# Linear attention and spectral mixing: attention batches written one ahead, transposes over head pairs, weights fetched later

## The chip, the cores and the metric

The kernel runs on one core of one Trainium2 chip. The metric is device time in microseconds (us) of one execution; lower is better. Where rows come from the hardware profiler, they are of one profiled execution of the kernel before.

## What is computed

The inputs q, k, v have shape 8 x 8 x 576 x 64 (batch, head, sequence, head size), the spectral weights `w_r` and `w_i` 64 x 512 x 512, the channel weights `w_ch` 512 x 512, all float32. The output is 8 x 576 x 512 float32.

```python
def phi(x):
    return np.where(x > 0, x, np.exp(x) - 1.0) + 1.0
q_p, k_p = (phi(q), phi(k))
kv = np.einsum('bhsd,bhse->bhde', k_p, v)
z = np.sum(k_p, axis=2)
num = np.einsum('bhsd,bhde->bhse', q_p, kv)
den = np.einsum('bhsd,bhd->bhs', q_p, z)[..., None] + 1e-06
x = num / den                      # heads side by side: 8 x 576 x 512
X = np.fft.rfft(x, axis=1)         # the first 64 modes are kept
Yr = einsum('bmd,mde->bme', Xr, w_r) - einsum('bmd,mde->bme', Xi, w_i)
Yi = einsum('bmd,mde->bme', Xr, w_i) + einsum('bmd,mde->bme', Xi, w_r)
y = np.fft.irfft(Y, n=S, axis=1)
u = x + y
out = u + np.maximum(u @ w_ch, 0.0)
```

## The kernel before

The program has three parts that follow one another.

**The attention part** (lines 128 to 294) loops over the 8 batches. For each it loads q, k and v (`q16`, `k16`, `v16`: 512 rows of the sequence, cast to half precision by the DMA, issued by POOL) and the last 64 rows (`q_t`, `k_t` in float32, issued by SP; `v16t`). VectorE and ScalarE form phi: a minimum with zero on DVE (L177), an exponential on ACT (L178), and one fused instruction on DVE, (x + 1) max e (L179); L182 to L184 do the same for the 64 tail rows. Then four head pairs follow. For each pair TensorE sums k'v into `kv_ps` (L206, 5 matmuls for each head), DVE copies it (`kv_sb`, L213), TensorE transposes q' into `qT_ps` (L219 and L222, 5 transposes for each head, each writing 64 partitions), ACT copies that (`q_pT`, L225 and L226), TensorE forms numerator and denominator (`num_ps`, L236 and L242), and DVE divides into `x_main` and `x_tail` (L251 to L259). At the batch's end ACT casts x to half precision (`x16m`, `x16t`), TensorE applies a Fourier matrix in five matmuls (`fft`, L273 and L276), ACT copies the result (`xr_sb`), and eight small transposes (`xtps`, L284) bring it into `xt_c`, from which DVE and ACT copy out twice each (L290 to L294).

**The spectral part** (L301 to L355) multiplies, for each of 64 modes, the batch rows of `xt_c` by `w_r` (L317) and `w_i` (L326): 128 weight tiles of 512 x 512, 0.5 MB each in half precision, all issued by POOL (L118, L120) into a pool with `bufs=7`. Every one of these matmuls reads all batches of `xt_c`, so the first stands behind the last batch's attention. `NPREF = 4` modes (8 tiles) are asked for within the batch loop, at batches 0, 2, 4 and 6.

**The last part** (L358 to L396) applies the inverse Fourier matrix (`inv_sb`), adds x, transposes (`utps`, L373), multiplies by `w_ch` (L380) and stores.

The code is written batch by batch, but a scheduler sets the order on each engine when the program is built, by priority and by which buffers are free; each engine then takes its instructions strictly in that order and waits where one isn't ready. POOL's queue counts too: a DMA that waits for a buffer holds up all that stand behind it. Most tiles of the batch loop have two buffers, `q_t`, `k_t`, `v16t` and `scr_t` one. `num_ps`, `fft` and `xtps` share four PSUM buffers.

Of the kernel before, what the change touches and what calls it, by code (L numbers as in the profile page):

```python
# [11 lines left out]
F32 = mybir.dt.float32  # L12
F16 = mybir.dt.float16
BF16 = mybir.dt.bfloat16
# [14 lines left out]
def _fft_consts(S: int, NM: int):  # L29
# [21 lines left out]
    inv = np.concatenate([inv, inv], axis=0)  # L51
# [4 lines left out]
def kernel(  # L56
# [15 lines left out]
    NB = 4  # L72
# [27 lines left out]
    nc.sync.dma_start(out=inv_sb, in_=inv_dr.ap())  # L100
# [15 lines left out]
    def _w_load(kk: int):  # L116
        wr = wpool.tile([128, NDC, D], BF16, tag="w", bufs=7, name=f"wr{kk}")
        nc.gpsimd.dma_start(out=wr, in_=moe_w_r[kk].rearrange("(dc p) e -> p dc e", p=128))  # L118
        wi = wpool.tile([128, NDC, D], BF16, tag="w", bufs=7, name=f"wi{kk}")
# [3 lines left out]
    with (  # L123
# [4 lines left out]
        for b in range(B):  # L128
            if b % 2 == 0 and b // 2 < NPREF:
                w_pref[b // 2] = _w_load(b // 2)  # L130
            q16 = qkv.tile([128, 2, H, 2, Dh], F16, tag="q16", bufs=2, name=f"q16_{b}")
            k16 = qkv.tile([128, 2, H, 2, Dh], F16, tag="k16", bufs=2, name=f"k16_{b}")
            v16 = qkv.tile([128, 2, H, 2, 72], F16, tag="v16", bufs=2, name=f"v16_{b}")
            q_t = qkv.tile([ST, H, Dh], F32, tag="q_t", bufs=1, name=f"q_t{b}")
            k_t = qkv.tile([ST, H, Dh], F32, tag="k_t", bufs=1, name=f"k_t{b}")
            v16t = qkv.tile([ST, H, 72], F16, tag="v16t", bufs=1, name=f"v16t{b}")

            for c in range(2):
                nc.gpsimd.dma_start(
                    out=q16[:, c],  # L140
                    in_=q[b, :, c * 256 : (c + 1) * 256, :].rearrange(
                        "h (s2 par) d -> s2 h (par d)", par=2
                    ),
                )
# [284 lines left out]
```

## Time and profile before

| | |
|---|---|
| six runs, median (lowest to highest) | 594.03 us (593.13 to 595.7) |
| the profiled execution, its own time | 595.7 us |
| its span in the trace | 593.7 us |
| first spectral matmul | 172.98 us |
| last weight tile's matmuls | 491.03 us |
| PE / DVE / ACT busy over the span | 71% / 35% / 22% |

The median is 0.3 us above the span and 1.7 us below the profiled execution's own time. The three parts are read apart, since each has its own limit: the attention part up to 173 us, the weights' stretch up to 491 us, and the last part. Differences between spans stand for differences between times.

### The profile page before, as it was taken

The numbers are of one execution on the slowest core, as the hardware profiler recorded it, in microseconds if no ns is written. First come the engines' busy times: TensorE is split into PE (matmuls) and PEld (weight loads), VectorE is DVE, ScalarE is ACT, GpSimd is POOL, SyncE is SP. The second block draws the span as 40 slices with busy tenths as digits, with TensorE's granted clock in tenths as the row PEclk, the third lists the DMA queues.
The fourth block names the chain that finished last, engine by engine and source line by source line (L and its number), as shares of the span: only waits on it lengthen the run. The fifth ranks groups of instructions, "written<-read, shape, count | busy, mean of one in ns | idle before, by whom it ended". The sixth has DMA issues, their size and how long they took to land.

```text
span 593.7 us, 5577 instructions
## 1 busy us (share of the span) xinstructions
PE 420.0 (71%) x1976; PEld 168.9 (28%) x1976; DVE 209.8 (35%) x529; ACT 131.7 (22%) x218; POOL 158.4 (27%) x205
## 2 busy tenths in 40 slices
PE   0378799999855665656666666767676664999885
PEld 0255465655521111111111111111111111323442
DVE  1485977777511101110110100311011103576653
ACT  1346666665420000000000000000000001502673
POOL 6656444330014222222322222222222200000000
PEclk9999999999997667676766555575655665867998
DMA  9999998983009999999999999999999990004444
GB/s 158 168 186 185 181 169 73 123 78 31 1 8 194 206 206 206 206 206 207 206 206 206 209 210 210 207 206 206 206 207 206 206 183 10 13 13 161 167 173 141
DMA packets 155243, 94.21 MB, mean 159 GB/s; under 512 B 83280, under 2 KB 150480, under 8 KB 155216
## 3 DMA queue, kind: packets, MB, share of 16 engines
q0 software_dynamic: 138896, 80.75, 95.9%
q1 hardware_dynamic: 16320, 13.12, 8.0%
q8 instruction: 15, 0.25, 0.2%
q14 instruction: 12, 0.10, 0.0%
HBM read 164.10 MB, written 9.44 MB: 292 GB/s over the span
## 4 chain that ended last, share of the span: by engine, by line
DMA 55%; PE 27%; issue 10%; DVE 4%; ACT 2%; POOL 1%; SPq 0%; DVEq 0%; POOLq 0%; ACTq 0%
DMA wi<-in_moe_w_i_dram 25%; DMA wr<-in_moe_w_r_dram 22%; PE e L380 6%; DMA q<-in_q_dram 5%; PE y L361 5%; PE P L326 3%; PE qT L219 3%; PE P L317 2%; DMA k<-in_k_dram 2%; PE kvp L206 2%; PE fft L273 1%; PE utp L373 1%; PE num L236 1%; ACT ut L377 1%; PE qT L222 1%
## 5 line engine op out<-in xcount | busy, mean ns | idle before, releaser
L317 PE MATMUL P<-wr,xt_c 128*16 128x512 bf16 x256 | 112.7, 594 | 56.6 <-DMA wr<-in_moe_w_r_dram 55.6
L336 DVE CAST ystage<-P 16x512 bf16<-16x512 f32 x64 | 43.9, 687 | 279.3 <-PE P L326 232.6
L326 PE MATMUL P<-wi,xt_c 128*16 128x512 bf16 x256 | 103.2, 550 | 52.6 <-DMA wi<-in_moe_w_i_dram 52.6
L370 ACT CAST u<-x_main 128x512 f16<-128x512 f32 x32 | 19.1, 624 | 329.7 <-DVE x_main L368 329.6
L120 POOL DMA_DIRECT2D wi<-in_moe_w_i_dram x64 | 47.5, 743 | 138.2 <-PE P L317 138.2
L118 POOL DMA_DIRECT2D wr<-in_moe_w_r_dram x64 | 48.0, 750 | 104.0 <-PE P L326 94.4
L317 PEld LDWEIGHTS <-xt_c 128*16 128x16 bf16 x256 | 30.1, 123 | 138.3 <-issue 115.3
L326 PEld LDWEIGHTS <-xt_c 128*16 128x16 bf16 x256 | 32.2, 126 | 125.2 <-issue 121.0
L219 PE MATMUL qT<-id,qp 128*64 128x128 f16 x256 | 40.1, 312 | 26.9 <-DVE qp L179 23.9
L380 PE MATMUL e<-wch,ut 128*128 128x512 f16 (+1 forms) x160 | 42.5, 406 | 5.7 <-ACT ut L377 4.1
L361 PE MATMUL y<-yg,inv_sb 64*128 64x512 bf16 (+1 forms) x80 | 32.3, 517 | 7.7 <-DMA yg<-ystage 6.5
L152 POOL DMA_DIRECT2D v<-in_v_dram x32 | 28.4, 899 | 28.3 <-PE kvp L206 22.2
L219 PEld LDWEIGHTS <-qp 128*64 128x64 f16 x256 | 25.8, 158 | 31.0 <-DVE qp L179 23.9
L178 ACT ACTIVATE scr<-scr 128x2048 f16<-128x2048 f16 x16 | 30.6, 1910 | 10.5 <-DVE scr L177 10.5
L377 ACT COPY ut<-utp 128x512 f16<-128x512 f16 (+1 forms) x40 | 20.5, 545 | 43.8 <-PE e L380 22.4
L388 DVE SCALAR_TENSOR_TENSOR osb<-e,x_main 128x512 f32<-128x512 f32 x32 | 22.1, 691 | 21.9 <-PE e L380 21.9
L206 PE MATMUL kvp<-v,kp 128*64 128x65 f16 x256 | 26.3, 249 | 3.4 <-DVE kp L179 3.4
L368 DVE TENSOR_TENSOR x_main<-x_main,y 128x512 f32<-128x512 f32 x32 | 21.7, 687 | 13.1 <-PE y L361 12.9
L225 ACT COPY qpT<-qT 128x512 f16<-128x512 f16 x32 | 18.8, 587 | 32.6 <-PE num L242 16.6
L253 DVE TENSOR_TENSOR x_main<-num,rdm 128x256 f32<-128x256 f32 x64 | 25.6, 400 | 0.2 <-DVE rdm L251 0.2
L380 PEld LDWEIGHTS <-ut 128*128 128x128 f16 (+1 forms) x160 | 14.5, 104 | 27.4 <-ACT ut L377 9.7
L206 PEld LDWEIGHTS <-kp 128*64 128x64 f16 x256 | 18.3, 150 | 10.1 <-DVE kp L179 3.7
(54 smaller groups left out, 360.9 us busy)
## 6 DMA issues: line engine op xcount, KB each, us to landing
wr<-in_moe_w_r_dram POOLq DMA_DIRECT2D x64, 512.0 KB, 15.6
wi<-in_moe_w_i_dram POOLq DMA_DIRECT2D x64, 512.0 KB, 15.6
out_dram<-osb SPq DMA_DIRECT2D x32, 256.0 KB
q<-in_q_dram POOLq DMA_DIRECT2D x16, 256.0 KB, 9.4
k<-in_k_dram POOLq DMA_DIRECT2D x16, 256.0 KB, 9.3
v<-in_v_dram POOLq DMA_DIRECT2D x32, 128.0 KB, 8.1
yg<-ystage SPq DMA_DIRECT2D x128, 8.0 KB
q_t<-in_q_dram SPq DMA_DIRECT2D x8, 128.0 KB
```

The costliest lines, as they stand in the source:

```text
L118: nc.gpsimd.dma_start(out=wr, in_=moe_w_r[kk].rearrange("(dc p) e -> p dc e", p=128))
L120: nc.gpsimd.dma_start(out=wi, in_=moe_w_i[kk].rearrange("(dc p) e -> p dc e", p=128))
L152: nc.gpsimd.dma_start(out=v16[:, c, :, par, :Dh], in_=v[b, :, c * 256 + par : (c + 1) * 256 : 2, :].rearrange("h s2 d -> s2 h d"),)
L178: nc.scalar.activation(out=scr16, in_=scr16, func=AF.Exp)
L206: nc.tensor.matmul(kv_ps[po : po + 64, :], lhs, rhs, start=(step == 0), stop=(step == 4),)
L219: nc.tensor.transpose(qT_ps[po : po + 64, j, :], q_p16[:, c, h, par, :], id16[:, :128])
L317: nc.tensor.matmul(p1[mo : mo + 16, :], xa[:, dc], wr[:, dc, :], start=(dc == 0), stop=False, tile_position=(0, mo),)
L326: nc.tensor.matmul(p1[mo : mo + 16, :], xb[:, dc], wi[:, dc, :], start=False, stop=(dc == NDC - 1), tile_position=(0, mo),)
L336: nc.vector.tensor_copy(out=ystage[mo : mo + 16, gg, :], in_=p1[mo : mo + 16, :])
L361: nc.tensor.matmul(yps[:rows, :], inv_sb[:NM, ri, j * 128 : j * 128 + rows], yg[b][:, ri, :], start=(ri == 0), stop=(ri == 1),)
L377: nc.scalar.copy(out=ut[:, :, :rows], in_=utps[:, :, :rows])
L380: nc.tensor.matmul(eps[:rows, :], ut[:, dc, :rows], wch16[:, dc, :], start=(dc == 0), stop=(dc == NDC - 1),)
```

## The change

- **Order of the source.** The loop runs one round longer. Round bb writes loads and phi of batch bb, and then the head pairs, the Fourier step and `xt_c` of batch bb - 1, through a `stash`.
- **Weights.** The eight early weight tiles are asked for in rounds 4 to 7, behind that round's q, k and v, and the pool has `bufs=8`, so that all eight have a buffer.
- **phi.** k comes before q. The fused instruction becomes two, an add of one (L192, L196 of the changed file) and a maximum with the exponential (L193, L197). `q_p16` is laid out as (c, par, head, d), so q's add and maximum come in four parts of 512 elements. `scr_t` is in half precision with two buffers, `v16t` has two.
- **Transposes.** With the two heads of a pair side by side in `q_p16`, one transpose covers both: 5 for a pair, over 128 columns, in place of 10 over 64 (L231 and L234 of the changed file).
- **inv.** The inverse matrix is no longer stored and loaded twice over; only the first 64 partitions were read.

```diff
-    inv = np.concatenate([inv, inv], axis=0)
...
-        wr = wpool.tile([128, NDC, D], BF16, tag="w", bufs=7, name=f"wr{kk}")
+        wr = wpool.tile([128, NDC, D], BF16, tag="w", bufs=8, name=f"wr{kk}")
...
-        for b in range(B):
-            if b % 2 == 0 and b // 2 < NPREF:
-                w_pref[b // 2] = _w_load(b // 2)
+        stash = {}
+        for bb in range(B + 1):
+            if bb < B:
+                b = bb
...
+                if b >= B - NPREF:
+                    w_pref[b - (B - NPREF)] = _w_load(b - (B - NPREF))
...
-                nc.vector.scalar_tensor_tensor(
-                    out=om, in0=fm, scalar=1.0, in1=scr16, op0=ALU.add, op1=ALU.max
-                )
+                    for om, fi, si in parts:
+                        nc.vector.tensor_scalar_add(out=om, in0=fi, scalar1=1.0)
+                        nc.vector.tensor_tensor(out=om, in0=om, in1=si, op=ALU.max)
...
+            if bb >= 1:
+                b = bb - 1
+                q_p16, k_p16, q_pt16, k_pt16, v16, v16t = stash.pop(b)
...
-                        nc.tensor.transpose(
-                            qT_ps[po : po + 64, j, :], q_p16[:, c, h, par, :], id16[:, :128]
+                        nc.tensor.transpose(
+                            qT_ps[:, j, :], q_p16[:, c, par, h0 : h0 + 2, :].rearrange("p h d -> p (h d)"), id16[:, :128]
```

What the scheduler makes of it shows at two places. The first is POOL's queue of DMAs in the attention part. `wr2`, `wi2` and so on are weight tiles, a number behind `q16`, `k16`, `v16` is the batch, and the last number only names the buffer. Before, with the weights of two modes already ahead of it (`wr0` and `wi0` at the very start):

```order
L139 DMA q16_3_911<-in_q_dram 128x8x128
L118 DMA wr2_1177<-in_moe_w_r_dram 128x4x512
L145 DMA k16_3_912<-in_k_dram 128x8x128 x2
L120 DMA wi2_1179<-in_moe_w_i_dram 128x4x512
L118 DMA wr3_1713<-in_moe_w_r_dram 128x4x512
L299 DMA wch16_68<-in_moe_w_ch_dram 128x4x512
L160 DMA v16t2_650<-in_v_dram 64x8x64
L152 DMA v16_3_913<-in_v_dram 128x8x64 x4
L139 DMA q16_4_1181<-in_q_dram 128x8x128 x2
L139 DMA q16_5_1447<-in_q_dram 128x8x128 x2
L145 DMA k16_4_1182<-in_k_dram 128x8x128 x2
L145 DMA k16_5_1448<-in_k_dram 128x8x128 x2
```

Now, with batches 0 to 2, q and k of batches 3 and 4, and the tiles `wr0`, `wi0`, `wr1`, `wi1` and `wr2` ahead of it:

```order
L151 DMA v16_3_666<-in_v_dram 128x8x64 x4
L159 DMA v16t3_669<-in_v_dram 64x8x64
L119 DMA wi2_1459<-in_moe_w_i_dram 128x4x512
L144 DMA k16_5_1181<-in_k_dram 128x8x128 x2
L117 DMA wr3_1717<-in_moe_w_r_dram 128x4x512
L119 DMA wi3_1719<-in_moe_w_i_dram 128x4x512
L313 DMA wch16_68<-in_moe_w_ch_dram 128x4x512
L138 DMA q16_5_1180<-in_q_dram 128x8x128 x2
L151 DMA v16_4_922<-in_v_dram 128x8x64 x4
L159 DMA v16t4_925<-in_v_dram 64x8x64
L144 DMA k16_6_1441<-in_k_dram 128x8x128 x2
L138 DMA q16_6_1440<-in_q_dram 128x8x128 x2
```

All eight early weight tiles and `wch` now stand ahead of v of batch 4. Before, `wi3` stood behind the last batch's loads, where it waited for a buffer.

The second place is DVE between the division of batch 2 and that of batch 3. `kvs`, `rm` (`rdm` before) and `n` (`num`) carry batch and pair. Before:

```order
L179 SCALAR_TENSOR_TENSOR qp4_1200<-q16_4_1181,scr16_4_1204 128x2048
L177 TENSOR_SCALAR scr16_5_1470<-q16_5_1447 128x2048
L184 SCALAR_TENSOR_TENSOR kpt3_933<-k_t3_915,scr_t3_935 64x512
L177 TENSOR_SCALAR scr16_4_1204<-k16_4_1182 128x2048
L290 COPY xt_c_92<-xtps2_898 128x4x64
L213 CAST kvs3_0_951<-kvp3_0_949 128x65
L213 CAST kvs3_1_1002<-kvp3_1_1000 128x65
L182 TENSOR_SCALAR scr_t4_1205<-q_t4_1184 64x512
L251 RECIPROCAL rdm3_0_0_987<-num3_0_0_975 128x4
```

Now:

```order
L192 TENSOR_SCALAR qp4_943<-q16_4_920 128x512 x3
L197 TENSOR_TENSOR kpt4_946<-kpt4_946,scr_t4_948 64x512
L192 TENSOR_SCALAR qp4_943<-q16_4_920 128x512
L194 TENSOR_SCALAR scr_t4_948<-q_t4_923 64x512
L196 TENSOR_SCALAR qpt4_945<-q_t4_923 64x512
L228 CAST kvs3_0_974<-kvp3_0_972 128x65
L228 CAST kvs3_1_1020<-kvp3_1_1018 128x65
L189 TENSOR_SCALAR s16_5_1207<-k16_5_1181 128x2048
L193 TENSOR_TENSOR qp4_943<-qp4_943,s16_4_947 128x512
L304 COPY xt_c_92<-xtps2_907 128x4x64
L193 TENSOR_TENSOR qp4_943<-qp4_943,s16_4_947 128x512 x3
L197 TENSOR_TENSOR qpt4_945<-qpt4_945,scr_t4_948 64x512
```

The parts of phi now stand as short instructions around the copies, and three of q's four maxima stand behind the copy of `xtps`. On PE, 8 matmuls of k'v stood between a batch's `fft` and its `xtps` in most batches before, and 19 do now; and k'v and q' of a batch's first two pairs stand ahead of the `fft` of the batch before it. From the spectral part on, the order on every engine is the same in both kernels.

## Rows read from the trace of the kernel before

**Rows 1.** The page's slices: 40 equal parts of the span (14.8 us each).
```profile
DMA  9999998983009999999999999999999990004444
GB/s 158 168 186 185 181 169 73 123 78 31 1 8 194 206 206 206 206 206 207 206 206 206 209 210 210 207 206 206 206 207 206 206 183 10 13 13 161 167 173 141
```

**Rows 2.** Stretches: length, busy of PE, PEld, DVE, ACT, POOL, PE's granted clock, DMA, GB/s.
```profile
0.00:89.00 89.00, 53.96 (x454) 35.61 (x454) 54.59 (x160) 43.14 (x61) 50.18 (x62) 1.00 1.69 175
89.00:172.98 83.98, 71.14 (x614) 45.13 (x613) 57.36 (x226) 46.65 (x78) 18.54 (x22) 1.00 0.61 54
172.98:491.03 318.05, 209.74 (x508) 56.07 (x508) 41.20 (x60) 0.00 (x0) 89.64 (x121) 0.62 1.21 201
491.03:593.70 102.67, 85.16 (x404) 32.11 (x403) 56.62 (x84) 41.90 (x80) 0.00 (x0) 0.80 0.30 98
```

**Rows 3.** The chain that ended last, in order of time: start, length, what.
```profile
175.14 5.86 DMA wi<-in_moe_w_i_dram
...
475.43 15.56 DMA wi<-in_moe_w_i_dram
```

**Rows 4.** POOL in order of time: start, length, instruction, idle ahead and releaser.
```profile
175.14 0.76 POOL L120 DMA_DIRECT2D wi<-in_moe_w_i_dram  x1 [29.39 <-PE P L317]
```

**Rows 5.** Busy time over one batch, from one `fft` to the next.
```profile
102.05:118.82 16.77, 15.52 (x134) 10.00 (x134) 12.73 (x49) 11.09 (x19) 6.79 (x9) 1.00 1.26 114
```

**Rows 6.** PE in order of time: the first `fft`, that batch, the seventh `fft`.
```profile
50.29 1.89 PE L273 MATMUL fft<-x16m,fwd_sb 128*128 128x512 f16 x4
...
102.05 1.89 PE L273 MATMUL fft<-x16m,fwd_sb 128*128 128x512 f16 x4
...
104.40 0.65 PE L206 MATMUL kvp<-v,kp 128*64 128x65 f16 x8
...
108.95 0.43 PE L206 MATMUL kvp<-v,kp 128*64 128x65 f16 x4
...
109.49 0.43 PE L206 MATMUL kvp<-v,kp 128*64 128x65 f16 x4
...
117.31 0.63 PE L219 MATMUL qT<-id,qp 128*64 128x128 f16 x4
...
118.06 0.63 PE L219 MATMUL qT<-id,qp 128*64 128x128 f16 x4
...
152.37 1.89 PE L273 MATMUL fft<-x16m,fwd_sb 128*128 128x512 f16 x4
```

**Rows 7.** PE in the last part, at transposes of 128 columns.
```profile
502.72 0.61 PE L373 MATMUL utp<-id,u 128*128 128x128 f16 x4
503.26 1.03 PE L361 MATMUL y<-yg,inv_sb 64*128 64x512 bf16 x2
```

**Rows 8.** The stretch around those, columns as in rows 2.
```profile
495.00:505.00 10.00, 5.24 (x17) 1.45 (x17) 3.38 (x6) 2.40 (x5) 0.00 (x0) 0.50 0.07 13
```

**Rows 9.** DVE within that batch: phi's instructions, and one pair's division.
```profile
108.48 0.68 DVE L177 TENSOR_SCALAR scr<-q 128x2048 f16<-128x2048 f16 x1
...
113.72 0.18 DVE L251 RECIPROCAL rdm<-num 128x4 f32<-128x4 f32 x1
...
114.94 0.16 DVE L251 RECIPROCAL rdm<-num 128x4 f32<-128x4 f32 x1
...
116.14 2.27 DVE L179 SCALAR_TENSOR_TENSOR kp<-k,scr 128x2048 f16<-128x2048 f16 x1
```

**Rows 10.** PE at the end of the attention part.
```profile
167.50 1.86 PE L273 MATMUL fft<-x16m,fwd_sb 128*128 128x512 f16 x4 [3.90 <-ACT x16m L268]
...
172.98 1.86 PE L317 MATMUL P<-wr,xt_c 128*16 128x512 bf16 x4 [0.87 <-ACT xt_c L294]
```

**Rows 11.** A weight issue on POOL, and DVE at the same moment.
```profile
46.22 1.14 POOL L118 DMA_DIRECT2D wr<-in_moe_w_r_dram  x1 [0.56 <-DMA k<-in_k_dram]
...
46.34 0.70 DVE L177 TENSOR_SCALAR scr<-q 128x2048 f16<-128x2048 f16 x1
```

More of the change, by code (lines that the diff above doesn't have):

```diff
@@ L99 @@
     nc.sync.dma_start(out=fwd_sb, in_=fwd_dr.ap())
-    nc.sync.dma_start(out=inv_sb, in_=inv_dr.ap())
+    nc.sync.dma_start(out=inv_sb[:NM], in_=inv_dr.ap())
     x_main = [
@@ L266 @@
-            x16m = sA.tile([128, NB, D], F16, tag="x16m", bufs=1, name=f"x16m{b}")
-            x16t = sA.tile([128, D], F16, tag="x16t", bufs=1, name=f"x16t{b}")
-            nc.scalar.copy(out=x16m, in_=x_main[b])
-            nc.scalar.copy(out=x16t[:ST, :], in_=x_tail[b][:ST, :])
-            xr_sb = sA.tile([128, D], BF16, tag="xr_sb", bufs=1, name=f"xrsb{b}")
-            ps_t = psA.tile([128, D], F32, tag="num_ps", bufs=4, name=f"fft{b}")
-            for j in range(NB):
+                    nc.scalar.copy(out=q_pT[:, :NB, :], in_=qT_ps[:, :NB, :])
@@ new lines @@
+                    nc.scalar.copy(out=q_pT[:, NB, :ST], in_=qT_ps[:, NB, :ST])
+                    num_ps = [
+                        psA.tile(
+                            [128, 5, Dh + 1], F32, tag="num_ps", bufs=4, name=f"n{b}_{hp}_{hh}"
+                        )
+                        for hh in range(2)
+                    ]
+                    for j in range(NB + 1):
+                        for hh in range(2):
+                            po = hh * 64
+                            if j < NB:
+                                nc.tensor.matmul(
+                                    num_ps[hh][:, j, :],
+                                    q_pT[po : po + 64, j, :],
+                                    kv_sb[po : po + 64, :],
+                                )
+                            else:
+                                nc.tensor.matmul(
+                                    num_ps[hh][:ST, NB, :],
+                                    q_pT[po : po + 64, NB, :ST],
+                                    kv_sb[po : po + 64, :],
+                                )
@@ new lines @@
+                x16m = sA.tile([128, NB, D], F16, tag="x16m", bufs=1, name=f"x16m{b}")
+                x16t = sA.tile([128, D], F16, tag="x16t", bufs=1, name=f"x16t{b}")
+                nc.scalar.copy(out=x16m, in_=x_main[b])
+                nc.scalar.copy(out=x16t[:ST, :], in_=x_tail[b][:ST, :])
+                xr_sb = sA.tile([128, D], BF16, tag="xr_sb", bufs=1, name=f"xrsb{b}")
+                ps_t = psA.tile([128, D], F32, tag="num_ps", bufs=4, name=f"fft{b}")
+                for j in range(NB):
+                    nc.tensor.matmul(
+                        ps_t, fwd_sb[:, j, :], x16m[:, j, :], start=(j == 0), stop=False
+                    )
```

249 lines of the change are left out of this document (117 added, 132 removed).

## The prediction

> **What bounds the kernel now.** I read the slices first [rows 1]: the DMA engines are full for six slices, fall away up to the twelfth, are full again for the weights, and are half busy at the end. The stretches [rows 2] say why there are three parts. From 173 to 491 us the weights arrive at 201 GB/s while PE waits for them; the chain of waits runs there from one weight tile to the next, from the issue at 175.14 to the last arrival at 475.43 + 15.56 = 491.0 [rows 3]. That is 121 tiles in 315.9 us, 2.61 us each. The issue at 175.14 had waited 29.39 us for PE's first spectral matmul [rows 4]: seven buffers were full, and the stream could not go on before the attention part had ended. So the total is the end of the attention part, plus the tiles that are then still to come, plus some 103 us of last part.
>
> The attention part has two halves [rows 2]. Up to 89 us the DMA engines are full (175 GB/s). After that they are mostly idle (54 GB/s), and each batch takes 16.77 us from one `fft` to the next, of which PE is busy 15.52, DVE 12.73 and ACT 11.09 [rows 5]. So PE sets that pace. From the last `fft` to the first spectral matmul it is 172.98 - 167.50 = 5.5 us [rows 10].
>
> **The change, part by part.**
>
> *Transposes.* Before, one head's five take 118.06 - 117.31 = 0.75 us, so a batch's 8 heads 6.0 [rows 6]. The nearest row for a transpose of 128 columns is in the last part: four take 503.26 - 502.72 = 0.54 us [rows 7], at a granted clock of 0.50, the lower level [rows 8]. I take that one, since it doesn't flatter; with 0.2 for the tail's, a pair costs 0.73 and a batch 2.9. PE's work falls from 15.5 to 12.4 us a batch. The bounds are 0 (two narrow ones cost as much as a wide one) and 3.5.
>
> *phi.* At 128 x 2048 the one-input half-precision instruction takes 0.68 us, of which some 0.08 overlap the next one, and the fused two-input one 2.27 [rows 9]. The add is of the first kind: 0.60. The maximum has no row; its bounds are 0.60 and 2.2. I take 1.15, the geometric middle, since it has one operation for each element like the first and two inputs like the second. Then k costs 1.75 in place of 2.2. q's four parts have a fixed cost of some 0.07 each, 4 x (0.20 + 0.34) = 2.2, as before. The tails about cancel. DVE's work is then 12.3 to 13.2 us a batch; I take 13.0. With the maximum at 2.2 it would be 15.5.
>
> On this price the Trainium skill, "VectorE: DVE Perf Modes", section "The perf-mode tier table", has half-precision `tensor_tensor` at two elements a cycle and `tensor_scalar` at four (1224 and 693 ns for 2048). The second agrees with the 0.68 here; no row here shows the first. By that rule the maximum would take 1.2, and the rival in which it takes 2.2 would fall away.
>
> *The order.* DVE and PE now carry almost the same work, and their queues are taken in order, so I walk one batch through the new order, from the moment that DVE ends the division of batch b. PE's last `num` ended some 2.0 earlier (a pair's division is 114.94 - 113.72 = 1.22 [rows 9], the rest is my estimate of its lead). PE then has two pairs' k'v of the next batch (0.54 a head [rows 6], 2.2), two pairs' transposes (1.5), the `fft` (104.40 - 102.05 = 2.35 [rows 6]), 19 k'v matmuls (2.1) and `xtps` (0.4): 6.5 to 7.1 us after that moment. DVE reaches its copy of `xtps` after 5.5 us of phi work and waits there, 1.6. What is queued behind that copy is q's last three maxima and the next batch's division. Work 13.0, this wait 1.6, and about nine hand-overs of 0.1: 15.5 us a batch in place of 16.77. PE is no longer what sets it, so of the 3.1 us saved there 1.3 arrive.
>
> *Loads.* No weights stand ahead of the first batch, but all eight tiles and `wch` now stand ahead of v of batch 4, and k'v of batch 4 stands ahead of `fft` 3 on PE. Up to the end of that v the queue holds, by the tiles' sizes, 4.9 MB (batches 0 to 2), 4.3 (q, k of 3 to 5, v of 3 and 4), 4.2 (weights), 0.5 (`wch`), and SP's 1.9 (tails, constants): 15.8 MB. At the 175 GB/s of the first 89 us [rows 2] it lands at 90 us. Then k'v and transposes of two pairs (3.7) lead to `fft` 3 at 93.7. The rest doesn't bind before that: were the first `fft` no earlier than now (50.29 [rows 6]), three batches of 15.5 would give 96.8; I expect it some 8 us earlier, since two tiles fewer stand ahead of the first loads (5.2 us at 2.61) and k comes first, so 89. The loads of batches 5 to 7 (1.9 MB each, some 11 us) come faster than 15.5.
>
> *The end.* `fft` 6 is at 93.7 + 3 x 15.5 = 140.2, and 2.2 later since all k'v of batch 7 stands ahead of it: 142.4. Before, the last interval was 167.50 - 152.37 = 15.1 [rows 6, 10]; without those 2.2 and some 1.6 of phi's wait it is 11.3, so `fft` 7 is at 153.7, and the first spectral matmul 5.5 later at 159.2. Gain: 13.8.
>
> *The stream.* It starts with that matmul, as before, and has 120 tiles to bring, not 121: 2.6 us. Nothing of the earlier start is given back, since the tiles come at a rate that the DMA engines set [rows 2]. The order from there on is unchanged: 0. The smaller `inv` is 0.15 MB, under 1 us at 175 GB/s and within the 90.
>
> Sum: 594.03 - 13.8 - 2.6 = **577.6 us**. It is a difference of spans, taken from the median; the profiled execution's own time is 1.7 above that.
>
> **The rivals.**
>
> *Engines overlap better (faster).* DVE's wait goes, because PE runs ahead further than I walked, and the pace is 13.2; v of batch 4 lands at 86 (184 GB/s, as near the 186 of slices 3 and 4 [rows 1]). Then 86 + 3.7 + 39.6 + 2.2 + 11.3 + 5.5 = 148.3, which is 24.7 earlier, and the time is 566.7. For it speaks that PE's lead is an estimate; against it that two engines so evenly loaded seldom run without waits, and that even now each has 1 to 4 us of them [rows 5].
>
> *Little gain in pace.* The maximum runs at one element a cycle (DVE 15.5), or wide transposes cost what narrow ones did (PE 15.5): 17.0 a batch, the first spectral matmul at 163.7, and 582.1. The earlier start remains.
>
> *Issue is starved (no change).* The POOL issue at 46.22 took 1.14 us, against 0.76 at 175.14, while DVE ran its one-input instruction [rows 4, 11]; the change adds more of that kind. If all 44 or so issues ahead of batch 4's v took 0.38 longer and nothing hid it, 17 us would go: 594.6. POOL was busy 50.18 of those 89 us [rows 2], so most of it should be hidden. The Trainium skill, "SBUF — State Buffer", section "SBUF: two separate sides", names this lock of the port that DVE and GpSimd share and speaks against the change by it; the row agrees in direction, 0.38 us for one issue.
>
> *Slower: DVE becomes the bound outright.* q's parts are cut into runs of 64, and if both add and maximum of them go at one element a cycle (0.6 each, 4.8) and k's maximum too (2.8 with its add), DVE has 17.4 and with waits the pace is 19.1. With the first `fft` at 45, 45 + 6 x 19.1 + 19 = 178.6: 5.6 later, less 2.6, 597.0. It decides from 18.9 us a batch. Against it: L177 is a row of the fast kind, and runs of 64 change only its pattern.
>
> **How the numbers follow.** My forecast has 0.52, better overlap 0.20, little gain in pace 0.20, starved issue 0.04, slower 0.04. To hold 8 in 10 the range takes the forecast, most of the second and most of the third: 566 to 586. Faster by over 0.3% (about what a measurement of this kernel can tell from no change) holds the first three and a little of the fourth: 0.93; within 0.3%: 0.03; slower: 0.04.
>
> **What would show it.** In the trace of the changed kernel: the first spectral matmul near 159; `fft` to `fft` 15.5 after the fourth, with DVE waiting some 1.6 for `xtps`; batch 4's k'v waiting for its v up to about 90; the maximum of k near 1.2; four transposes of a pair within 0.55; tiles at 2.61 and 120 of them. I am wrong if v of batch 4 isn't waited for, if the maximum is far from 1.2, or if the last part's length moves by more than 2 us.

## The result and the profile after

The changed kernel takes **576.94 us** (median of 8 runs, 576.67 to 578.63) against 594.33 us of the kernel before (16 runs, 592.92 to 596.01): a ratio of 0.971, with a 95% interval of 0.9696 to 0.9723. The forecast was 577.6. The profiled execution's span is 574.9 us, where it was 593.7.

The slices of the page, in the same 40 pieces as [rows 1]: DMA in tenths, then GB/s. The valley between the two full stretches begins and ends a slice earlier.

```profile
DMA  9999999960089999999999999999999990004544
GB/s 148 169 172 195 182 193 170 151 43 0 1 135 206 207 206 206 206 207 206 206 206 207 210 210 209 206 206 206 206 206 207 206 149 10 14 13 171 179 166 146
```

The stretches that answer to [rows 2], cut at the issue that restarts the weight stream and at its last arrival (columns: length; busy us and instructions of PE, PE's weight loads, DVE, ACT, POOL; granted clock; DMA share; GB/s):

```profile
0.00:89.00 89.00, 49.63 (x449) 31.77 (x450) 66.01 (x259) 51.09 (x76) 56.21 (x64) 1.00 1.64 176
89.00:159.64 70.64, 52.97 (x463) 31.69 (x464) 43.99 (x207) 37.34 (x63) 19.00 (x21) 0.62 0.81 68
159.64:473.23 313.59, 216.96 (x505) 55.78 (x502) 41.20 (x60) 0.00 (x0) 88.90 (x120) 0.56 1.22 203
473.23:574.90 101.67, 84.96 (x404) 32.06 (x403) 56.68 (x84) 41.97 (x80) 0.00 (x0) 0.80 0.30 99
```

The chain of waits of the changed kernel at three places (start, us, what), answering to [rows 3]:

```profile
83.20 9.26 DMA v16t<-in_v_dram
92.46 0.04 issue
92.50 0.51 PE kvp L221 x4
...
159.64 5.53 DMA wr<-in_moe_w_r_dram
...
455.05 18.14 DMA wi<-in_moe_w_i_dram
473.19 0.04 issue
473.23 1.88 PE P L340 x4
```

The span is 18.8 us shorter, where the medians differ by 17.4: the profiled execution before ran 1.4 above its median, the one after 0.3 below. The 18.8 are three pieces. The first spectral matmul is at 157.48, not 172.98: 15.5. The stream now needs 473.19 - 159.64 = 313.6 us for 120 tiles, still 2.61 each, where it was 315.9 for 121 [rows 3]: 2.3. The last part takes 101.7 us, where it was 102.7 [rows 2]: 1.0, which no part of the change asked for.

In the attention part the `fft` starts are at 43.5, 58.9, 74.3, 95.7, 109.5, 124.0, 139.6 and 152.0. Four intervals of the changed kernel, in the columns of the stretches above:

```profile
95.70:109.50 13.80, 11.66 (x115) 7.35 (x115) 10.56 (x49) 7.99 (x15) 8.25 (x10) 0.72 2.02 170
109.50:124.02 14.52, 12.62 (x114) 8.05 (x114) 13.09 (x59) 10.68 (x18) 4.20 (x5) 0.50 1.12 85
124.02:139.59 15.57, 13.53 (x133) 8.88 (x133) 10.53 (x53) 9.58 (x17) 0.00 (x0) 0.61 0.01 2
139.59:152.00 12.41, 5.79 (x55) 2.96 (x55) 5.92 (x36) 4.60 (x9) 0.00 (x0) 0.50 0.01 1
```

A normal batch is the second: 14.52 us where it was 16.77 [rows 5]. PE's busy time fell from 15.52 to 12.62; DVE's is 13.09 and now the largest. The interval of 21.4 us from 74.3 to 95.7 is so long because PE waits for v of batch 4, 6.6 us in five waits. The first and the last two of them (PE's timeline; in brackets the idle time ahead of an instruction, and what ended it):

```profile
89.51 0.22 PE L221 MATMUL kvp<-v,kp 128*64 128x65 f16 x1 [4.47 <-DMA v<-in_v_dram]
...
92.06 0.21 PE L221 MATMUL kvp<-v,kp 128*64 128x65 f16 x1 [0.53 <-DMA v<-in_v_dram]
92.50 0.21 PE L221 MATMUL kvp<-v16t,kpt 64*64 64x65 f16 x1 [0.23 <-DMA v16t<-in_v_dram]
```

phi in the changed kernel, by groups (busy us in all, mean ns of one, idle before): maximum and add of q (four parts a batch) and of k.

```profile
L193 DVE TENSOR_TENSOR qp<-qp,s 128x512 f16<-128x512 f16 x32 | 11.9, 417 | 0.2 <-ACT s L190 0.2
L193 DVE TENSOR_TENSOR kp<-kp,s 128x2048 f16<-128x2048 f16 x8 | 9.7, 1210 | 0.0
L192 DVE TENSOR_SCALAR qp<-q 128x512 f16<-128x512 f16 x32 | 8.6, 309 | 8.2 <-DMA q<-in_q_dram 8.2
L192 DVE TENSOR_SCALAR kp<-k 128x2048 f16<-128x2048 f16 x8 | 6.0, 750 | 0.0
```

### The profile page after: what moved, and what is told of

Same layout as the page of the kernel before. It is cut to its first block, busy times and chain, and to the rows that moved or that the text cites. A ratio compares the mean times of both kernels' runs of the same rounds, so it can differ in the third digit from the quotient of the medians.

```text
span 574.9 us, 5349 instructions
## 1 busy us (share of the span) xinstructions
PE 404.5 (70%) x1816; PEld 151.3 (26%) x1816; DVE 207.9 (36%) x609; ACT 130.4 (23%) x218; POOL 164.1 (29%) x205
## 4 chain that ended last, share of the span: by engine, by line
DMA 54%; PE 23%; issue 10%; DVE 8%; ACT 2%; POOL 1%; SPq 0%; DVEq 0%; POOLq 0%; ACTq 0%
DMA wr<-in_moe_w_r_dram 46%; PE e L394 7%; PE y L375 5%; PE P L331 5%; DMA wi<-in_moe_w_i_dram 3%; DMA k_t<-in_k_dram 2%; PE kvp L221 2%; DMA v16t<-in_v_dram 2%; DMA k<-in_k_dram 1%; PE utp L387 1%; ACT ut L391 1%; DVE x_main L267 1%; DVE qp L193 1%; DVE kp L193 1%; PE qT L231 1%
## 5 line engine op out<-in xcount | busy, mean ns | idle before, releaser
L340 PE MATMUL P<-wi,xt_c 128*16 128x512 bf16 x256 | 112.6, 593 | 48.7 <-DMA wi<-in_moe_w_i_dram 48.7
L350 DVE CAST ystage<-P 16x512 bf16<-16x512 f32 x64 | 43.9, 687 | 277.0 <-PE P L340 222.9
L151 POOL DMA_DIRECT2D v<-in_v_dram x32 | 30.7, 971 | 22.2 <-PE kvp L221 8.2
L190 ACT ACTIVATE s<-s 128x2048 f16<-128x2048 f16 x16 | 30.5, 1903 | 14.7 <-DVE s L189 14.7
L267 DVE TENSOR_TENSOR x_main<-n,rm 128x256 f32<-128x256 f32 x64 | 25.6, 400 | 0.2 <-DVE rm L265 0.2
L237 ACT COPY qpT<-qT 128x512 f16<-128x512 f16 x32 | 18.8, 588 | 22.3 <-PE n L256 18.6
L231 PE MATMUL qT<-id,qp 128*128 128x128 f16 x128 | 19.5, 305 | 5.9 <-DVE qp L193 3.1
L250 PE MATMUL n<-kvs,qpT 64*128 64x65 f16 x256 | 16.2, 234 | 7.6 <-DVE x_tail L273 4.3
L394 PEld LDWEIGHTS <-ut 128*128 128x128 f16 (+1 forms) x160 | 14.5, 104 | 26.4 <-ACT ut L391 9.7
```

Source lines behind the costliest of these rows:

```text
L151: nc.gpsimd.dma_start(out=v16[:, c, :, par, :Dh], in_=v[b, :, c * 256 + par : (c + 1) * 256 : 2, :].rearrange("h s2 d -> s2 h d"),)
L190: nc.scalar.activation(out=scr16, in_=scr16, func=AF.Exp)
L267: nc.vector.tensor_tensor(out=x_main[b][:, :, h * Dh : (h + 1) * Dh], in0=num_ps[hh][:, :NB, :Dh], in1=rden_m.unsqueeze(2).broadcast_to([1 ...
L340: nc.tensor.matmul(p1[mo : mo + 16, :], xb[:, dc], wi[:, dc, :], start=False, stop=(dc == NDC - 1), tile_position=(0, mo),)
L350: nc.vector.tensor_copy(out=ystage[mo : mo + 16, gg, :], in_=p1[mo : mo + 16, :])
L394: nc.tensor.matmul(eps[:rows, :], ut[:, dc, :rows], wch16[:, dc, :], start=(dc == 0), stop=(dc == NDC - 1),)
```

## The experiments

The theory: the attention part ends when v of batch 4 has come, plus three batches at a pace in which DVE's work and its waits for PE add up, plus the last batch; each us there is a us of the total. The rivals: a pace that PE alone or DVE alone sets, and a start that is carried through whatever the loads do. All runs in one table; the ratio is to the kernel before, run beside it, and "pace" is the fifth interval between two `fft`s.

| run | us | ratio (95%) | first `fft` | pace | first spectral matmul |
|---|---|---|---|---|---|
| before | 594.33 | 1 | 50.3 | 16.8 | 173.0 |
| changed | 576.94 | 0.971 (0.9696 to 0.9723) | 43.5 | 14.5 | 157.5 |
| weights held behind v | 568.93 | 0.9577 (0.9545 to 0.9609) | 43.6 | 14.5 | 151.4 |
| weights early, as before | 582.38 | 0.9812 (0.979 to 0.9834) | 53.2 | 14.5 | 163.6 |
| v16t in one buffer | 589.39 | 0.9929 (0.9906 to 0.9951) | 43.1 | 14.7 | 170.7 |
| narrow transposes | 589.74 | 0.9931 (0.9904 to 0.9958) | 48.6 | 16.9 | 170.2 |
| phi fused | 583.03 | 0.9815 (0.9777 to 0.9854) | 44.8 | 16.7 | 163.8 |
| batch by batch | 577.68 | 0.9721 (0.9688 to 0.9753) | 37.1 | 15.6 | 159.7 |
| before, eight buffers | 592.55 | 0.9978 (0.996 to 0.9996) | 50.0 | 16.8 | 173.4 |
| before, new arithmetic | 591.67 | 0.9961 (0.9943 to 0.9979) | 42.8 | 16.4 | 170.2 |
| merged tails | 589.34 | 0.9926 (0.9908 to 0.9944) | 43.7 | 14.0 | 171.9 |
| held, merged tails | 583.63 | 0.983 (0.9803 to 0.9856) | 44.5 | 14.0 | 165.8 |
| held, `xtps` earlier | 567.91 | 0.9571 (0.9548 to 0.9594) | 43.4 | 13.8 | 148.4 |
| held, `xtps` first | 570.29 | 0.9605 (0.958 to 0.9631) | 43.3 | 14.4 | 150.9 |

The fifth interval stands for a batch in the steady stretch, except in four runs whose intervals are uneven: batch by batch, before with new arithmetic, and the two with merged tails.

### Is v of batch 4 what is waited for?

The weight tiles are tied behind v of their batch on POOL's queue:

```diff
-                nc.gpsimd.dma_start(
+                last_v = nc.gpsimd.dma_start(
                     out=v16t[:, :, :Dh], in_=v[b, :, 512:, :].rearrange("h s d -> s h d")
                 )
                 if b >= B - NPREF:
-                    w_pref[b - (B - NPREF)] = _w_load(b - (B - NPREF))
+                    with tc.issue_after(last_v.ins):
+                        w_pref[b - (B - NPREF)] = _w_load(b - (B - NPREF))
```

The same is done with the load of `wch`, behind the last v.

> The changed kernel with its eight early weight tiles and the channel weight held back on the issuing queue, each pair behind v of its own batch, so that only q, k and v stand ahead of v of batch 4. Theory (PE waited 9.3 us, 83.2 to 92.5, for v of batch 4 because 4.7 MB of weights stood ahead of it): that wait goes, fft 3 comes one pace after fft 2, at 74.3 + 15.4 = 89.7 in place of 95.7, the first spectral matmul is some 6 us earlier, near 151.5, and the time is near 571. Rival (the wait only hid that DVE and PE had not kept up; batches run at 15.4 us while loads run, and the two fast batches after the wait, 13.8 and 14.5, were backlog): fft 3 near 89.7 but then 15.4 a batch, so the gain is 6 - 2.5 = 3.5 us, near 573.5. Second rival (the late weights now come too late for the first spectral matmuls): no gain, 577 or more.

It came to 568.93, 8.0 us less than changed, and the wait is gone: `fft` 3 is at 88.1 (89.7 expected), and the batches around it run at one pace. (The 9.3 us of the expectation are the flight of one load in the chain; PE itself stood idle for 6.6.) Two of them (columns as above), and all of DVE's waits in the second (who waits for what: us in all, times, longest):

```profile
73.56:88.09 14.53, 12.62 (x113) 8.05 (x113) 13.10 (x59) 10.68 (x18) 10.32 (x11) 1.00 1.78 182
88.09:102.62 14.53, 12.62 (x113) 8.05 (x113) 13.10 (x59) 10.68 (x18) 8.01 (x9) 1.00 1.68 182
```

```profile
DVE xt_c L305 <- PE xtps L299: 1.4, 1, 1.4
```

The attention part ends 6.05 us earlier, as the theory said. The rival's 15.4 a batch is not there: with loads at 182 GB/s the pace is the 14.5 that it was at 85 GB/s. DVE's 13.10 of work and 1.4 of waiting fill the 14.53, so it waits for nothing but PE. The stream takes the same 313.5 us (153.60 to 467.13); 1.5 more came off the last part, of which below.

The other way round, the tiles asked for early as before the change:

```diff
+                if b % 2 == 0 and b // 2 < NPREF:
+                    w_pref[b // 2] = _w_load(b // 2)
                 q16 = qkv.tile([128, 2, H, 2, Dh], F16, tag="q16", bufs=2, name=f"q16_{b}")
...
-                if b >= B - NPREF:
-                    w_pref[b - (B - NPREF)] = _w_load(b - (B - NPREF))
```

> The changed kernel with its eight early weight tiles asked for at the head of batches 0, 2, 4 and 6, as before the change (eight buffers). Two tiles stand ahead of batch 0's loads, so the first fft should come some 5 us later than 43.5; the bytes ahead of batch 4's v stay the same. Theory (v of batch 4 and the bytes ahead of it set the end of the attention part, not the first fft): v of batch 4 still lands near 90, fft 3 stays near 96, and the time is within 2.5 us of the changed kernel, 575 to 579.5. Rival (the late first batch is carried through to the end): +5 us, 582.

The rival was right: 582.38. The theory's sentence on the bytes was true and beside the point, since the first `fft` slipped by 9.7 us, not 5, and past the moment at which v of batch 4 bound anything. PE's first wait in this run:

```profile
23.95 0.43 PE L221 MATMUL kvp<-v,kp 128*64 128x65 f16 x4 [23.95 <-DVE kp L193]
```

In the changed kernel PE's first wait ended at 18.0: 6.0 earlier, somewhat more than two tiles at 2.61. Most of the rest is a wait of DVE for k of batch 2, straight ahead of batch 0's last division, where DVE has no wait in the changed kernel:

```profile
48.69 0.69 DVE L189 TENSOR_SCALAR s<-k 128x2048 f16<-128x2048 f16 x1 [4.64 <-DMA k<-in_k_dram]
```

So the late weights earned 5.4 us of the total at the start, and cost 6.05 in the attention part by standing ahead of v of batch 4.

### Does the order of the loads rest on the second buffer of v16t?

```diff
-                v16t = qkv.tile([ST, H, 72], F16, tag="v16t", bufs=2, name=f"v16t{b}")
+                v16t = qkv.tile([ST, H, 72], F16, tag="v16t", bufs=1, name=f"v16t{b}")
```

> The changed kernel with v16t in one buffer, as before the change, all else as changed. Its load for batch b+1 can then be issued only when PE has done the last k'v of batch b, and in the changed order PE wants the first k'v of batch b+1 some 4.8 us after that (93.9 to 98.7 in the run with held weights), while a load takes 5 to 9 us to land. Theory (the second buffer of v16t is what the new order of PE rests on): PE waits 2 to 4.3 us in most batches, the first spectral matmul is 10 to 25 us later, 587 to 602. Rival (PE finds other work, or the load lands in time): within 2 us of the changed kernel, 575 to 579.

589.39, within the theory's range, but by another road: two long waits early, and from `fft` 3 on 14.6 to 14.7 a batch. Of this run, PE's two waits, then POOL's timeline and the chain:

```profile
71.00 0.21 PE L221 MATMUL kvp<-v16t,kpt 64*64 64x65 f16 x1 [14.58 <-DMA v16t<-in_v_dram]
...
89.22 0.21 PE L221 MATMUL kvp<-v16t,kpt 64*64 64x65 f16 x1 [3.69 <-DMA v16t<-in_v_dram]
```

```profile
55.39 0.69 POOL L159 DMA_DIRECT2D v16t<-in_v_dram  x1 [2.67 <-DMA wr<-in_moe_w_r_dram]
```

```profile
55.39 15.57 DMA v16t<-in_v_dram
```

With one buffer the small load must wait for PE, so in the built order it falls behind six weight tiles on POOL's queue. It is the place in the queue that costs 14.6 us, not the 64 KB. (That the one buffer is why it falls there is read from the two orders.)

### What sets the pace

Ten narrow transposes a pair again, the rest as changed:

```diff
-                    for j in range(NB):
-                        c, par = j // 2, j % 2
-                        nc.tensor.transpose(
-                            qT_ps[:, j, :], q_p16[:, c, par, h0 : h0 + 2, :].rearrange("p h d -> p (h d)"), id16[:, :128]
-                        )
+                    for hh in range(2):
+                        h = h0 + hh
+                        po = hh * 64
+                        for j in range(NB):
+                            c, par = j // 2, j % 2
+                            nc.tensor.transpose(
+                                qT_ps[po : po + 64, j, :], q_p16[:, c, par, h, :], id16[:, :128]
+                            )
...
```

> The changed kernel with ten narrow transposes a pair of heads (one head each) in place of five wide ones; all else as changed. It adds PE work of (40.1 - 19.5) / 8 = 2.6 us a batch, by the sums of the transposes in the two traces. Theory (PE and DVE together set the pace after batch 4's v has landed at about 92): over the four batches after it PE's extra work arrives for more than half, +5 to +8 us, near 583. Rival (DVE alone sets the pace, PE has room): under +2 us, near 578. Rival (PE alone sets it): +2.6 x 4.5 = 12 us, near 589.

And phi fused again (the tails' too):

```diff
-                        nc.vector.tensor_scalar_add(out=om, in0=fi, scalar1=1.0)
-                        nc.vector.tensor_tensor(out=om, in0=om, in1=si, op=ALU.max)
+                        nc.vector.scalar_tensor_tensor(
+                            out=om, in0=fi, scalar=1.0, in1=si, op0=ALU.add, op1=ALU.max
+                        )
...
```

> The changed kernel with add and maximum of phi fused again into one instruction, as before the change; all else as changed. By rows, k's add and maximum took 0.75 + 1.21 = 1.96 us against 2.27 fused, and q's four parts 4 x (0.31 + 0.42) = 2.9 against 2.3 to 2.5 fused, so DVE's work is about the same, 0.1 to 0.3 us a batch less with the fused form. Theory (work counts, not the mode): within 1 us of the changed kernel, 576 to 578. Rival (the fused form blocks POOL's issues or DVE's hand-overs for longer, and the split form was what brought the pace down): +4 us or more, 581.

Both missed the theory and came out at a rival: 589.74, a pace of 16.9, where the rival that PE alone sets the pace had 589, and 583.03, a pace of 16.7, where the rival that the split form was what brought the pace down had 581 or more. Two batches of the narrow run and one of the fused (columns as above):

```profile
99.20:116.12 16.92, 15.83 (x135) 10.21 (x134) 13.70 (x62) 10.79 (x18) 6.47 (x7) 1.00 1.56 132
116.12:133.03 16.91, 15.82 (x134) 10.20 (x134) 13.09 (x59) 10.79 (x18) 4.20 (x5) 1.00 0.62 51
```

```profile
94.75:111.41 16.66, 12.94 (x114) 7.82 (x114) 14.04 (x52) 10.71 (x18) 7.95 (x10) 1.00 2.01 168
```

DVE's waits in the first and the last of these, and between them PE's one wait in each batch of the narrow run:

```profile
DVE xt_c L307 <- PE xtps L301: 1.9, 1, 1.9
DVE rm L268 <- PE n L259: 1.3, 1, 1.3
```

```profile
PE n L253 <- DVE x_tail L276: 1.1, 1, 1.1
```

```profile
DVE xt_c L306 <- PE xtps L300: 2.0, 1, 2.0
DVE xt_c L309 <- PE xtps L300: 0.6, 1, 0.6
```

In each run DVE's work and its waits for PE add up to the interval: 13.10 + 1.4 = 14.5 with held weights, 13.70 + 1.9 + 1.3 = 16.9 narrow, 14.04 + 2.0 + 0.6 = 16.6 fused. That sum shows only that DVE waits for nothing but PE; whichever engine sets the pace, it comes out. What tells them apart is a batch with other work. In the narrow run DVE works 13.70 us in one batch and 13.09 in the next, and both take 16.9: its waits give way. PE's 15.8 and its one wait of 1.1 fill both. So there PE all but sets the pace, as the rival had it; the time is the rival's by other pieces, since `fft` 3 was already 3.5 us late. In the fused run PE has only 12.94 of work, and three batches with 14.16, 14.04 and 13.84 us of DVE's work all take 16.65: neither fills it alone. With held weights DVE's work is the same in every batch, so that run can't tell; the runs that move `xtps`, below, can. The fused form costs DVE little in work: q and k take (20.4 + 18.3) / 8 = 4.8 us a batch by its groups, against (11.9 + 8.6 + 9.7 + 6.0) / 8 = 4.5 split. The split add can run before ACT's exponential is ready, the fused instruction can't, and its built order is another; which of the two makes the longer batch was not separated.

The wide transposes over the fused phi run at 16.7 and the split phi over narrow transposes at 16.9, as long as before (16.8). Only both together give 14.5, and only in the new order of the source, as the next runs show.

### The source order, the arithmetic alone, the eighth buffer

The changed kernel, written batch by batch:

```diff
-        for bb in range(B + 1):
+        for bb in range(B):
...
-            if bb >= 1:
-                b = bb - 1
+            if True:
+                b = bb
```

> The changed kernel written batch by batch (phi of a batch straight ahead of its own heads, no phi of the next batch between), all else as changed. In the built order PE still does k'v of the next batch before the fft of this one, in part: two of its four heads' pairs are split round the fft. Theory (the order is made by the scheduler and the pools; the source order adds little): within 3 us of the changed kernel, 574 to 580. Rival (the written order is what lets DVE and PE overlap): pace back near 16.8 a batch, +8 us, 585.

577.68: the time is the theory's, the pace the rival's. The five intervals from the second `fft` to the seventh are 15.6, 15.5, 19.8, 15.6 and 17.5, on the mean 16.8, where they are 14.9 with held weights. The time comes out the same because the first `fft` comes at 37.1, 6.4 earlier, since on DVE q's phi of batch 1 now stands behind batch 0's division, not ahead of it, and because PE hardly waits for v of batch 4 (1.0 us).

The kernel before with only the new arithmetic (wide transposes, split phi with k first, half-precision tail scratch in two buffers):

```diff
-                nc.vector.scalar_tensor_tensor(
-                    out=om, in0=fm, scalar=1.0, in1=scr16, op0=ALU.add, op1=ALU.max
-                )
+                for om, fi, si in parts:
+                    nc.vector.tensor_scalar_add(out=om, in0=fi, scalar1=1.0)
+                    nc.vector.tensor_tensor(out=om, in0=om, in1=si, op=ALU.max)
...
```

> The kernel before, with its source order, its weight loads and its seven buffers, and only the arithmetic of the change: wide transposes and phi as add and maximum (half-precision tail scratch in two buffers, k ahead of q). The wide transposes alone over the fused phi gave 16.65 us a batch, the split phi alone over narrow transposes 16.9, and both in the source order batch by batch 15.5. Theory (the two are worth something only together; the pace does not need the new source order): some 15.5 a batch from a first fft near 50, the first spectral matmul near 164, about 9 us less than before, 585. Rival (the new order carries the pace): 16.7 a batch, 593 or more. Rival (order is worth nothing at all): 14.5 a batch, 578.

591.67, near the rival's 593: the arithmetic alone brings 2.3 us. Its five intervals are 17.0, 17.6, 16.9, 16.4 and 15.8, on the mean 16.7, the same as batch by batch. So both arithmetic edits in the old source order leave the pace at 16.7 to 16.8, and the new order is the third thing that the 14.5 needs, as both rivals said. The 14 us between the two runs in the old order are not a matter of pace: 9.7 have arisen by the second `fft` (55.2 against 64.9), and one tile less behind the attention part is 2.6. What batch by batch has beside this run are the late weights (5.4 us when undone in the changed kernel), the second buffer of v16t (12.5 there) and the eighth weight buffer; how they share the 9.7 was not taken apart.

The kernel before with eight weight buffers:

```diff
-        wr = wpool.tile([128, NDC, D], BF16, tag="w", bufs=7, name=f"wr{kk}")
+        wr = wpool.tile([128, NDC, D], BF16, tag="w", bufs=8, name=f"wr{kk}")
```

> The kernel before with eight weight buffers in place of seven, nothing else. Theory (each tile that is there before the first spectral matmul is one of 2.61 us less behind it): 2.6 us less than before, 0.9956 of it. Rival (the eighth tile only takes the loads' place in the attention part): no gain, 1.000. Rival (the stream's rate also gains by a deeper queue): more than 4 us, under 0.993.

0.9978, 1.3 us (0.2 to 2.4): the sign is the theory's, the size half of it. In the profiled executions the stream is 2.8 shorter, as it should be, and the first spectral matmul 0.4 later.

### Two things that should have been faster

The two tail inputs in one tile of 128 rows, in two buffers:

```diff
-                q_t = qkv.tile([ST, H, Dh], F32, tag="q_t", bufs=1, name=f"q_t{b}")
-                k_t = qkv.tile([ST, H, Dh], F32, tag="k_t", bufs=1, name=f"k_t{b}")
+                kq_t = qkv.tile([2 * ST, H, Dh], F32, tag="kq_t", bufs=2, name=f"kq_t{b}")
...
-                nc.sync.dma_start(out=q_t, in_=q[b, :, 512:, :].rearrange("h s d -> s h d"))
-                nc.sync.dma_start(out=k_t, in_=k[b, :, 512:, :].rearrange("h s d -> s h d"))
+                nc.sync.dma_start(out=kq_t[ST:], in_=q[b, :, 512:, :].rearrange("h s d -> s h d"))
+                nc.sync.dma_start(out=kq_t[:ST], in_=k[b, :, 512:, :].rearrange("h s d -> s h d"))
...
```

> The changed kernel with the two tail inputs of 64 rows (k_t, q_t) put into one tile of 128 rows, k in the lower and q in the upper half, in two buffers; the four tail instructions of phi are done once for both. The same bytes of memory. In the changed kernel the chain of waits holds two loads of k_t of 6.7 us one after the other at 16.8 and 24.3 us, with DVE waiting. Theory (v of batch 4 ends the first half, and it lands by the sum of the bytes ahead of it): the first fft comes earlier by up to 13 us, near 32 to 37, but batch 4's v still lands at about 89 to 92, fft 3 stays within 2 us of 95.7, and only DVE's saving of some 1 us a batch after it can show: 574 to 577. Rival (v of batch 4 was late because its issue waited for buffers that the late start kept): fft 3 moves with the first fft, 565 to 569.

> Both at once: the weights held back behind v as in the run with held weights, and the merged tail tile in two buffers. Theory (with the weights out of the way the start carries through): the first fft near 35, seven intervals of some 14 to 14.5, the first spectral matmul near 140 to 143, and 557 to 561. Rival (the first fft is bound by the loads of batch 0 and by phi, not by the tails): first fft 40 or later, 564 to 567. Rival (the loads of later batches become the bound: 1.9 MB a batch at 176 GB/s is 11 us, plus tiles): intervals above 15.5, 567 or more.

589.34 and 583.63: both are some 12 to 15 us slower than the kernels they start from, and the first `fft` did not move (43.7 and 44.5). The theory was wrong in both; the rival that the first `fft` is bound by other work was right on the `fft`, not on the time. Two things were read from the traces; no run undoes one of them alone. First, 13.5 us of the changed kernel's chain lay under the loads of `k_t`, but DVE itself was idle for them only 5.8, in two waits (its waits up to 60 us):

```profile
DVE scr_t L194 <- DMA k_t<-in_k_dram: 5.8, 2, 3.8
```

With those gone, DVE waits for q instead, 13.9 us up to the first `fft` where it was 8.2; its work up to there is 24.8, where it was 25.8. The merged tails without held weights:

```profile
DVE qp L185 <- DMA q<-in_q_dram: 13.9, 3, 6.3
```

Second, in the built order phi of a later batch now stands ahead of ready work in DVE's queue, and its input had not come: without held weights q of batch 5, ahead of what was left of batches 2 and 3 (17.6 us of idle time); with them k of batch 7, ahead of batches 3 and 4 (10.8). That more buffers are what lets the built order do this is argued. The run without held weights, DVE first, then POOL:

```profile
88.88 0.53 DVE L185 TENSOR_SCALAR qp<-q 128x512 f16<-128x512 f16 x2 [12.91 <-DMA q<-in_q_dram]
94.09 0.86 DVE L185 TENSOR_SCALAR qp<-q 128x512 f16<-128x512 f16 x2 [4.68 <-DMA q<-in_q_dram]
```

```profile
70.03 0.74 POOL L309 DMA_DIRECT2D wch<-in_moe_w_ch_dram  x1
71.15 0.89 POOL L137 DMA_DIRECT2D q<-in_q_dram  x1 [0.38 <-DVE rm L261]
...
85.08 0.88 POOL L137 DMA_DIRECT2D q<-in_q_dram  x1 [2.25 <-DMA wi<-in_moe_w_i_dram]
```

The two halves of that q stand on POOL's queue behind tiles and `wch`, the second as late as 85.08, and DVE stood still for those 17.6 us with ready work behind it; `fft` 3 came at 108.1.

Then the wait of 1.4 us itself, on the kernel with held weights:

```diff
+                    if hp == 3 and b > 0:
+                        es = tc.issue_after(last_xt.ins)
+                        es.__enter__()
                     for hh in range(2):
...
```

`last_xt` is the fourth transpose into `xtps`; the edge ends behind that pair's k'v. The second run has 2 in place of 3.

> The kernel with held weights (568.9), and on PE the first four transposes into xtps put ahead of the k'v of the next batch's last pair, not behind it; all other engines in the same order. There DVE waited 1.37 to 1.43 us a batch for xtps (pace 14.53, DVE busy 13.10). Theory (DVE's work and this wait make the pace, 13.10 + 1.43 = 14.53): the wait falls by one pair's k'v, 0.9 to 1.1, the pace to 13.5 to 13.7, over six or seven batches some 6 us, 562 to 564. Rival (the pace is a loop through PE's wait for DVE's division, 1.02, and the k'v that are put off make that longer): gain under 2 us, 567 or more.

> As the run before it, but the first four transposes into xtps ahead of both late pairs' k'v of the next batch, straight behind the fft. PE must then wait some 0.7 us for ACT's copy of the fft's output, with nothing to do beside it. Theory (DVE's work and its wait make the pace): DVE's wait goes to nearly 0, the pace to 13.2 to 13.5 (PE 12.62 + 0.7 = 13.3), 560 to 563, at or below the run before it. Rival (PE's extra wait comes back through its lead over DVE): slower than the run before it, 565 or more.

567.91 and 570.29: both times are the rivals' (567 or more, 565 or more), and neither can be told from the held kernel's 568.93 by its interval. But the first has its first spectral matmul 3.1 us earlier, half of what the theory had. Two of its batches (columns as above):

```profile
86.45:100.70 14.25, 12.77 (x114) 8.10 (x114) 14.10 (x59) 10.80 (x18) 9.08 (x10) 1.00 1.66 183
100.70:114.51 13.81, 12.77 (x114) 8.10 (x113) 13.50 (x59) 10.68 (x18) 8.86 (x10) 1.00 1.81 179
```

DVE's wait of 1.4 fell to 0.5 and less, and now the batches follow DVE's work: 14.25 at 14.10, 13.81 at 13.50. So the wait had been on the path, as the theory said. The rest of the 3.1 is missing because DVE's busy time itself grew, by 0.0 to 1.0 us in a batch, for a reason that I had not seen coming (last section); and the last part was 1.9 longer. With `xtps` first PE waits 0.9 for ACT's copy at each `fft`, and the batches take 14.4 with 13.36, 14.07 and 13.28 us of DVE's work alike: there PE and its waits for ACT set the pace.

## Why the prediction was right, step by step

*Transposes: right.* Four wide ones take 0.52 to 0.54 us up to the start of the next instruction (0.54), a batch's PE work is 12.62 (12.4 forecast).

*phi: right.* The forecast counts an instruction without the 0.08 by which it overlaps the next one. So counted, k's maximum takes 1.13 (1.15) and its add 0.67 (0.60). For q's parts, two rows of the normal batch:

```profile
109.97 0.68 DVE L192 TENSOR_SCALAR qp<-q 128x512 f16<-128x512 f16 x3
114.64 1.09 DVE L193 TENSOR_TENSOR qp<-qp,s 128x512 f16<-128x512 f16 x3
```

One add is (0.68 - 0.08) / 3 = 0.20 and one maximum (1.09 - 0.08) / 3 = 0.34, so the four parts take 2.2, as forecast. The fixed cost of 0.07, for which no row stood, comes out of them too: (4 x 0.20 - 0.60) / 3. DVE's work is 13.09 (13.0). On the maximum the Trainium skill, "VectorE: DVE Perf Modes", section "The perf-mode tier table", has 1224 ns for bf16; the rows agree, for fp16 (1210).

*Order walk: the wait right, the pace a us too long.* DVE waits 1.4 for `xtps` (1.6). The nine hand-overs of 0.1 that I added are not there: DVE's work and that wait fill the interval to under 0.1. This is the term that was mis-sized: three intervals and batch 7's k'v took 43.9 us, not 48.7. Of the 4.8, 3.0 are the pace. The other 1.8 are the first interval (13.80, with 10.56 us of DVE's work, since DVE had run ahead while PE waited for v) and batch 7's k'v, which made the third 1.05 longer, not 2.2.

*Loads: 2 us late.* v of batch 4 held PE until 92.5, not 90, at the rate that was assumed (176 GB/s): 16.3 MB had moved by then, not 15.8. Its last piece, `v16t`, was issued at 83.20 and took 9.26. `fft` 3 is at 95.7, not 93.7. That this is what bound is shown by the run with held weights. That the first `fft` "doesn't bind before that" was true by 7.6 us only: with the weights held `fft` 3 is at 88.1. The run with early weights, whose first `fft` slips by 9.7, shows it bind.

*The end.* The last interval is 12.4, not 11.3; from there to the first spectral matmul 5.5, as forecast. Together 2.0 - 4.8 + 1.1 = -1.7: 157.5, not 159.2. The errors half cancel, so the 0.7 us by which the total was missed flatters the working: that is luck. It also compares a median with a sum of spans. In spans the forecast was 16.4 us of gain and 18.8 were measured: 1.7 more in the attention part, 1.0 more in the last part, 0.3 less in the stream.

*Stream: right,* 120 tiles at 2.61. *Last part:* 1.0 shorter, forecast 0.

*Rivals.* The pace of 13.2 was reached in no run. "Little gain in pace" (17.0) is what the kernel would have had without either one of the two arithmetic changes, or with both in the old order of the source. DVE did become the engine with the most work, yet far from 18.9 a batch. What the starved issue costs the changed kernel was not separated; its price was real (last section). Two sums of the rivals are off by their own terms: with the maximum at 2.2, DVE's work is 13.0 + 1.05 + 4 x 0.26 = 15.1, not 15.5, and with all parts at one element a cycle it is 13.0 + 2.6 + 1.05 = 16.7, not 17.4, which gives some 592.5 us, a little faster than before and not slower.

## What to carry to other kernels

Where two engines take turns, the busy time of one and its waits for the other give the interval whichever of them sets it. Look for batches in which that busy time differs, and see whether the interval follows. Two edits that are worth nothing singly may be worth much together, and only in an order that lets the engines overlap. A time that a theory forecast is no proof of its pace: read the pace by itself. On POOL's in-order queue the place of a load decided, not its size (64 KB took 15.6 us behind six tiles): put what is needed first ahead of what only has to be there later, and after any change of buffers or source order read again what the built order put in front of whom. A long DMA in the chain of waits is not the time that an engine lost to it; that stands in the engine's own idle time.

## What the hardware showed

*The price of POOL's issues on DVE.* [rows 11] had a POOL issue take 0.38 us longer beside a one-input DVE instruction. It works the other way as well. DVE in the run with held weights, and in the run with `xtps` earlier, where DVE no longer waits:

```profile
90.06 0.41 DVE L197 TENSOR_SCALAR qpt<-q_t 64x512 f16<-64x512 f32 x1
90.66 0.67 DVE L190 TENSOR_SCALAR s<-k 128x2048 f16<-128x2048 f16 x1
```

```profile
88.59 0.78 DVE L197 TENSOR_SCALAR qpt<-q_t 64x512 f16<-64x512 f32 x1
89.56 1.05 DVE L190 TENSOR_SCALAR s<-k 128x2048 f16<-128x2048 f16 x1
```

And POOL in the second run:

```profile
88.04 2.08 POOL L144 DMA_DIRECT2D k<-in_k_dram  x2 [0.53 <-DVE qp L193]
90.16 1.80 POOL L138 DMA_DIRECT2D q<-in_q_dram  x2
```

0.78 - 0.41 = 0.37 and 1.05 - 0.67 = 0.38, while POOL issues. This is where a part of the won wait went: DVE was busy 14.10 of 14.25 us in this batch, against 13.10 of 14.53, and its eleven one-input instructions on phi are 1.0 us longer together, the others together not. It is not the price of every meeting. In this run's attention part 44 one-input instructions (TENSOR_SCALAR) begin during a POOL issue; 14 of them are longer by over 0.1 us, none by more than 0.38 (in the changed kernel 11 of 36, none by more than 0.50). Of the 44 that don't begin during one none is longer, and of the 184 two-input ones (TENSOR_TENSOR) none either. The Trainium skill, "SBUF — State Buffer", section "SBUF: two separate sides", has a port that the two engines share under a lock for a whole instruction; the rows agree in kind, but most meetings cost nothing here.

*The length of the last part* lay between 99.9 and 102.7 us in these kernels, though no run touches it and its instructions stand in the same order before and after the change. Why was not tried. A difference of a few us between two of these runs is therefore read from the attention part.

*The granted clock* reads 1.00 in the whole attention part before [rows 2, 5] and 0.50 to 0.61 from 109.5 us on in the changed kernel, but the matmuls there are no slower. A batch's PE work is 12.62 us at 1.00 (held weights) and at 0.50 (changed). The four wide matmuls of an `fft` take 1.89 us before [rows 6], and in the changed kernel:

```profile
109.50 1.86 PE L287 MATMUL fft<-x16m,fwd_sb 128*128 128x512 f16 x4 [0.25 <-ACT x16m L282]
```

So the column alone was no evidence of a slower PE here.
